# Turning q and k with DMA transposes instead of TensorE, in a sparse-attention and GEGLU kernel

## The chip, the cores and the metric

The kernel runs on one core of one Trainium2 chip. The metric is device time in microseconds (us). Each kernel was executed several times and the median is given. Ratios are the mean time of one kernel's fast runs over that of the other's fast runs of the same rounds, so they are not quite the ratio of the quoted medians. Traces come from one profiled execution; it can lie 1% away from the median. The engines are PE (TensorE), DVE (VectorE), ACT (ScalarE), POOL (GpSimd) and SP (SyncE, which issues DMAs here).

## The reference, cut to what matters

```python
B, H, S, D = 4, 8, 768, 64                  # batch, heads, tokens, head size
k_sum = k.reshape(B, H, 24, 32, D).max(axis=3)      # block keys
v_sum = v.reshape(B, H, 24, 32, D).mean(axis=3)     # block values
scores = concat([masked(q @ k.T, |i-j| < 16), q @ k_sum.T + log(32)]) # scaled by 1/8
x = softmax(scores) @ concat([v, v_sum])            # then (B*S, 512)
ffn = (gelu(x @ w_gate) * (x @ w_val)) @ w_out      # 512 -> 1536 -> 512
out = x + sigmoid(x @ w_res) * ffn
```

## The kernel before

The work is cut into eight units, two halves of 384 tokens per batch. A unit is first twelve gate/value steps (`fo_step`), then the output matmuls, between which the attention of the next unit is done. Attention needs q and k with the head size on the partitions, so they have to be turned. The turning of the next batch is spread over the twelve steps of the current batch's second half.

```python
def load_qk(src, b, parts, name):      # 96 partitions, rows of 8 tokens x 64: 2 KB runs
    t = qk.tile([PP, H, PJ, D], BF16, tag=name, name=name)
    ...
    nc.gpsimd.dma_start(out=t[...], in_=src[b, ...].rearrange("h (p j) d -> p h (j d)", j=PJ))

def turn_pair(src, hp, pool, tag):     # 16 small PE transposes into one PSUM tile
    tp = pool.tile([128, PJ, PP], BF16, tag=tag, name="tp")
    for j in range(PJ):
        for hh in range(2):
            nc.tensor.transpose(tp[hh*64:hh*64+64, j, :], src[:, 2*hp+hh, j, :], ident[0:PP, 0:PP])
    return tp

def k_step(b, hp, pool, tag):
    tp = turn_pair(k_sb[b], hp, pool, tag)
    nc.scalar.copy(kw[:, 1:NT-1, 0:BAND]..., src)           # ACT: ten windows of 96 keys
    nc.vector.tensor_copy(kw[:, 0, ...], ...)               # DVE: the two edge windows
    nc.vector.tensor_copy(kw[:, NT-1, ...], ...)
    nc.vector.tensor_reduce(out=ks..., in_=kw..., op=ALU.max)   # block keys
    nc.vector.tensor_copy(kw[:, :, BAND:BAND+NB], ks...)

def q_step(b, hp, pool, tag):
    tp = turn_pair(q_sb[b], hp, pool, tag)
    nc.scalar.copy(qT[b % 2][hp]..., tp...)

def vsum_grp(b, pool, tag):            # block means of v: 12 matmuls, then 4 small transfers
    ...
    nc.vector.tensor_copy(vpart[:], vs[:])
    for g in range(4):
        nc.sync.dma_start(out=vsum[b % 2][96+6*g:102+6*g, :], in_=vpart[32*g:32*g+6, :])

for u in range(NU):
    b, half = u // 2, u % 2
    nb = b + 1
    if half == 0 and nb < B:
        k_sb[nb] = load_qk(k, nb, 1, "k_sb")
        q_sb[nb] = load_qk(q, nb, 1, "q_sb")
        v_loads(nb)                    # 12 transfers, rows of 64 elements
    for fo in range(FO):
        fo_step(st, gvT, fo)
        if half == 1 and nb < B:
            if fo == 1:   vsum_grp(nb, ps_t, "t"); vsum_bc(...)   # POOL copies
            elif fo < 6:  k_step(nb, fo - 2, ps_t, "t")           # cut
            elif fo < 10: q_step(nb, fo - 6, ps_t, "t")           # cut
    # ... output matmuls of unit u, attention of unit u+1
```

The pool `ps_t` has one buffer, and `fo_step` takes its two PSUM tiles from a pool of four.

The softmax here doesn't subtract the row's maximum and nothing guards it: scores larger than these inputs give would overflow.

## Time and profile before

The time is 314.01 us (median of 4 runs, 311.92 to 315.53). From the page, the span, the busy times, and the chain that ended last:

```profile
span 309.7 us, 6206 instructions
PE 273.7 (88%) x2584; PEld 148.7 (48%) x2584; DVE 171.5 (55%) x379; ACT 136.0 (44%) x200; POOL 81.4 (26%) x104
PE 66%; DMA 16%; POOL 7%; DVE 5%; issue 4%; ACT 1%; POOLq 0%; DVEq 0%
```

The average of 88% hides two kinds of stage. The next view is the table of stretches: from and to, length, busy us of each engine with its instruction count, the granted PE clock, a DMA share and GB/s. The stretches are the twelve gate steps of the units 1, 2, 3 and 5; the odd units are second halves.

```profile
69.70:99.90 30.20, 25.05 (x240) 12.86 (x237) 17.14 (x32) 12.48 (x21) 13.15 (x14) 0.89 1.01 100
113.70:129.70 16.00, 16.00 (x103) 9.38 (x102) 7.92 (x15) 5.98 (x13) 0.00 (x0) 1.00 0.06 24
143.50:167.40 23.90, 21.59 (x239) 11.93 (x236) 16.38 (x32) 12.38 (x21) 12.36 (x12) 1.00 0.43 76
...
211.00:235.10 24.10, 21.62 (x241) 11.96 (x240) 16.45 (x32) 12.41 (x21) 5.58 (x3) 1.00 0.05 16
```

A second half takes 24 us where a first half takes 16. The 8 us between them are the turns, the block sums, and about 2.3 us in which PE waits for the one turning buffer. The timeline of PE shows that wait: start, length, what, and in brackets the idle time before it and what ended it.

```profile
158.64 0.53 PE L171 MATMUL tp<-ident,q_sb 96*64 96x96 bf16 x16 [1.74 <-DVE kW_3_91 L184]
```

Before the two DVE copies that free the buffer, DVE copies the block keys of the pair before:

```profile
155.93 1.91 DVE L191 COPY kW_2_90<-ks 128x288 bf16<-128x288 bf16 x1
```

The same copy took 0.23 us for the first pair. The long one lies within the three block-sum copies of POOL (152.17 to 157.75 us).

The first change of batch takes 30.2 us, 6 us longer, since PE also waits 2.7 us for v there, and its clock is 0.89 in the mean. It comes while the weights and the loads of batch 1 still keep the DMA engines full, as the chain shows (start, length, what):

```profile
48.35 17.26 DMA q_sb<-in_q_dram
67.49 8.22 DMA vext_105<-in_v_dram
75.75 1.23 PE vs L209 x8
```

### The profile page before, as it was taken

What the parts mean: (1) busy time and instruction counts of PE and PEld (TensorE: products, weight loads), DVE (VectorE), ACT (ScalarE), POOL (GpSimd) and SP (SyncE); (2) the same over time, 40 slices, a digit from 0 to 9 for tenths busy, and PEclk for the clock granted to TensorE, in tenths of its full rate; (3) what the DMA queues carried; (4) which work ended last, traced back from release to release, by engine and by line L of the source; (5) the groups of instructions that cost most, each with busy time, mean ns of one, the idle gap of its engine ahead of it and who ended that gap; (6) DMA issues with size and microseconds to landing.
All of it is one profiled execution on the core that took longest, in us unless ns stands there. A gap on an engine that the chain in (4) does not pass through costs nothing.

```text
span 309.7 us, 6206 instructions
## 1 busy us (share of the span) xinstructions
PE 273.7 (88%) x2584; PEld 148.7 (48%) x2584; DVE 171.5 (55%) x379; ACT 136.0 (44%) x200; POOL 81.4 (26%) x104
## 2 busy tenths in 40 slices
PE   1555599996979999999979999999979999999993
PEld 0521355452445455554545556555445556455641
DVE  3540764383593574367773674377863764475423
ACT  2640223641456543544547443562646623643310
POOL 8628777241393400000392400000610000000000
PEclk9975789998799999999999999999999999999998
DMA  6994999999049950001049960011000110011001
GB/s 104 163 86 51 176 196 207 207 153 149 3 67 183 101 75 35 2 34 70 5 65 178 103 111 1 2 37 68 5 0 2 36 68 2 1 65 39 2 34 68
DMA packets 54987, 22.88 MB, mean 74 GB/s; under 512 B 37480, under 2 KB 51888, under 8 KB 54960
## 3 DMA queue, kind: packets, MB, share of 16 engines
q0 software_dynamic: 51360, 16.13, 78.1%
q1 hardware_dynamic: 3600, 6.37, 6.3%
q8 instruction: 20, 0.33, 0.5%
q14 instruction: 7, 0.06, 0.1%
HBM read 32.24 MB, written 6.29 MB: 124 GB/s over the span
## 4 chain that ended last, share of the span: by engine, by line
PE 66%; DMA 16%; POOL 7%; DVE 5%; issue 4%; ACT 1%; POOLq 0%; DVEq 0%
PE f L297 18%; PE g L273 16%; PE vv L277 15%; PE r L287 6%; DMA q_sb<-in_q_dram 6%; DMA vext_104<-in_v_dram 5%; DMA w_val<-in_moe_w_val_dram 3%; PE tp L171 3%; DMA vext_105<-in_v_dram 3%; PE ao L249 2%; DVE ks L187 2%; PE s L231 2%; PE xp L260 2%; DVE gvT L281 2%; PE vs L209 1%
## 5 line engine op out<-in xcount | busy, mean ns | idle before, releaser
L281 DVE TENSOR_TENSOR gvT<-ge,vv 128x384 bf16<-128x384 f32 x96 | 52.8, 550 | 60.4 <-PE vv L277 60.3
L280 ACT ACTIVATE ge<-g 128x384 f32<-128x384 f32 x96 | 47.3, 493 | 81.1 <-PE g L273 43.9
L273 PE MATMUL g<-xT,w_gate 128*128 128x384 bf16 x384 | 81.7, 332 | 0.0
L277 PE MATMUL vv<-xT,w_val 128*128 128x384 bf16 x384 | 79.1, 329 | 0.0
L297 PE MATMUL f<-w_out,gvT 128*128 128x512 bf16 x288 | 68.4, 379 | 0.0
L277 PEld LDWEIGHTS <-w_val 128*128 128x128 bf16 x384 | 38.0, 99 | 26.5 <-issue 2.7
L235 ACT ACTIVATE P<-s,bias_t 128x768 bf16<-128x768 f32 x32 | 28.9, 904 | 45.4 <-PE s L231 45.3
L273 PEld LDWEIGHTS <-w_gate 128*128 128x128 bf16 x384 | 35.5, 99 | 25.4 <-issue 4.4
L297 PEld LDWEIGHTS <-gvT 128*128 128x128 bf16 x288 | 27.3, 98 | 31.0
L238 DVE TENSOR_TENSOR P<-P,maskt 128x768 bf16<-128x768 bf16 x32 | 17.8, 556 | 20.4 <-ACT P L235 20.4
L221 POOL COPY vext_105<-vsum_107 32x2048 bf16<-32x2048 bf16 x6 | 11.2, 1897 | 56.2 <-DMA vsum_107<-vpart 56.2
L287 PE MATMUL r<-w_res,xT 128*128 128x512 bf16 x96 | 24.8, 380 | 0.0
L96 POOL DMA_DIRECT2D vext_105<-in_v_dram x24 | 18.2, 764 | 19.6 <-DMA q_sb<-in_q_dram 7.7
L221 POOL COPY vext_104<-vsum_106 32x2048 bf16<-32x2048 bf16 (+1 forms) x4 | 8.3, 2110 | 47.5 <-DMA vsum_106<-vpart 47.4
L96 POOL DMA_DIRECT2D vext_104<-in_v_dram x24 | 18.3, 767 | 9.1 <-PE vv L277 3.5
L302 DVE SCALAR_TENSOR_TENSOR th<-th,f 128x512 f32<-128x512 f32 x24 | 16.3, 680 | 7.0 <-PE f L297 7.0
L171 PE MATMUL tp<-ident,k_sb 96*64 96x96 bf16 x256 | 9.9, 229 | 9.9 <-DMA k_sb<-in_k_dram 6.4
L255 DVE TENSOR_TENSOR xn<-ao,rz 128x384 bf16<-128x384 f32 x32 | 17.8, 558 | 1.1
L290 ACT ACTIVATE th<-r 128x512 f32<-128x512 f32 x24 | 14.3, 596 | 8.8 <-PE r L287 8.3
L304 DVE SCALAR_TENSOR_TENSOR o<-th,xn 128x512 f32<-128x512 f32 x24 | 16.6, 692 | 0.8
L249 PEld LDWEIGHTS <-P 128*64 128x64 bf16 x384 | 9.1, 114 | 14.8 <-DVE P L238 5.9
L171 PE MATMUL tp<-ident,q_sb 96*64 96x96 bf16 x256 | 9.4, 222 | 6.6 <-DMA q_sb<-in_q_dram 3.0
(150 smaller groups left out, 221.6 us busy)
## 6 DMA issues: line engine op xcount, KB each, us to landing
out_dram<-o SPq DMA_DIRECT2D x24, 256.0 KB
k_sb<-in_k_dram POOLq DMA_DIRECT2D x3, 768.0 KB, 8.0
q_sb<-in_q_dram POOLq DMA_DIRECT2D x3, 768.0 KB, 12.0
vext_104<-in_v_dram POOLq DMA_DIRECT2D x20, 96.0 KB, 8.6
vext_105<-in_v_dram POOLq DMA_DIRECT2D x20, 96.0 KB, 11.8
w_gate<-in_moe_w_gate_dram POOLq DMA_DIRECT2D x6, 256.0 KB, 8.3
w_val<-in_moe_w_val_dram POOLq DMA_DIRECT2D x6, 256.0 KB, 8.9
w_out<-in_moe_w_out_dram POOLq DMA_DIRECT2D x3, 512.0 KB, 14.0
```

The costliest lines, as they stand in the source:

```text
L96: nc.gpsimd.dma_start(out=vext[b % 2][r0:r1, t, :, 0:D], in_=src)
L171: nc.tensor.transpose(tp[hh * 64:hh * 64 + 64, j, :], src[:, 2 * hp + hh, j, :], ident[0:PP, 0:PP])
L221: eng.tensor_copy(vext[b % 2][96:128, lo:hi, :, 0:D], src)
L235: nc.scalar.activation(P.rearrange("p a t q -> p a (t q)"), s[:, :, 0:TU], AF.Exp, scale=scale, bias=bias_t[:])
L238: nc.vector.tensor_mul(Pf, Pf, maskt.unsqueeze(1).to_broadcast([128, 2 * HT, QT]))
L255: nc.vector.tensor_mul(xn, ao[:, :, :, 0:D], rz.to_broadcast([128, NSUB, 2, D]))
L273: nc.tensor.matmul(g[:, 0:TU], w_gate[:, ko, fs], st["xT"][:, ko, :], start=(ko == 0), stop=(ko == KO - 1))
L277: nc.tensor.matmul(vv[:, 0:TU], w_val[:, ko, fs], st["xT"][:, ko, :], start=(ko == 0), stop=(ko == KO - 1))
L280: nc.scalar.activation(ge[:], g[:, 0:TU], AF.Gelu)
L281: nc.vector.tensor_mul(gvT[:, fo, :], ge[:], vv[:, 0:TU])
L287: nc.tensor.matmul(r[:], st["xT"][:, ko, ss], w_res[:, ko, :], start=(ko == 0), stop=(ko == KO - 1))
L297: nc.tensor.matmul(st["f"][:], gvT[:, fo, ss], w_out[:, fo, :], start=(fo == 0), stop=(fo == FO - 1))
```

## The change

The intent is to take the turning of batches 1 to 3 off PE, ACT and DVE. k and q are loaded in token order (rows of 64 elements), and 18 DMA transposes per batch, issued from SP, write them turned into their places. As SP is then busy, the four block-sum transfers move from SP to ACT. The pool `qk` goes from two buffers to one, so the next batch's loads have to wait for these transposes. Batch 0 is left as it was.

```diff
+    def load_nat(b):
+        kn = qk.tile([BAND, NT, H, D], BF16, tag="k_nat", name="k_nat")
+        nc.gpsimd.memset(kn[0:32, 0], 0.0)
+        nc.gpsimd.memset(kn[64:96, NT - 1], 0.0)
+        for t in range(NT):
+            ...
+            nc.gpsimd.dma_start(out=kn[r0:r0 + hi - lo, t], in_=k[b, :, lo:hi, :].rearrange("h p d -> p h d"))
+        qn = qk.tile([128, S // 128, H, D], BF16, tag="q_nat", name="q_nat")
+        for c in range(S // 128):
+            nc.gpsimd.dma_start(out=qn[:, c], in_=q[b, :, c * 128:(c + 1) * 128, :].rearrange("h p d -> p h d"))
+
+    def turn_k(b, lo, hi):                      # turn_q: the same, 6 pieces of 128 x 512
+        for t in range(lo, hi):
+            nc.sync.dma_start_transpose(out=kW_all[b % 2][:, :, t, 0:BAND],
+                                        in_=k_nat[b][:, t].rearrange("p h d -> p (h d)"))
...
             for g in range(4):
-                nc.sync.dma_start(out=vsum[b % 2][96 + 6 * g:102 + 6 * g, :],
+                nc.scalar.dma_start(out=vsum[b % 2][96 + 6 * g:102 + 6 * g, :],
...
-                k_sb[nb] = load_qk(k, nb, 1, "k_sb")
-                q_sb[nb] = load_qk(q, nb, 1, "q_sb")
+                load_nat(nb)
                 v_loads(nb)
...
                 if half == 1 and nb < B:
-                    if fo == 1:
+                    if fo == 0:
+                        turn_k(nb, 0, NT)
+                        turn_q(nb, 0, S // 128)
+                    elif fo == 2:
                         vsum_grp(nb, ps_t, "t")
...
-                    elif 2 <= fo < 2 + NP:
-                        k_step(nb, fo - 2, ps_t, "t")
-                    elif 2 + NP <= fo < 2 + 2 * NP:
-                        q_step(nb, fo - 2 - NP, ps_t, "t")
+                    elif 6 <= fo < 6 + NP:
+                        k_blocks(nb, fo - 6)    # the DVE reduction and copy of k_step
```

More of the change, by code (lines that the diff above doesn't have):

```diff
@@ L51 @@
     wpool = ctx.enter_context(tc.tile_pool(name="wpool", bufs=1))
-    qk = ctx.enter_context(tc.tile_pool(name="qk", bufs=2))
+    qk = ctx.enter_context(tc.tile_pool(name="qk", bufs=1))
     work = ctx.enter_context(tc.tile_pool(name="work", bufs=3))
@@ L66 @@
     warm = const.tile([128, 512], BF16, name="warm")
-    kW = [[const.tile([128, NT, 128], BF16, name=f"kW{i}_{p}") for p in range(NP)] for i in range(2)]
-    qT = [[const.tile([128, S], BF16, name=f"qT{i}_{p}") for p in range(NP)] for i in range(2)]
+    kW_all = [const.tile([128, NP, NT, 128], BF16, name=f"kW{i}") for i in range(2)]
+    qT_all = [const.tile([128, NP, S], BF16, name=f"qT{i}") for i in range(2)]
+    kW = [[kW_all[i][:, p] for p in range(NP)] for i in range(2)]
+    qT = [[qT_all[i][:, p] for p in range(NP)] for i in range(2)]
     vext = [const.tile([128, NT, H, D + 1], BF16, name=f"vext{i}") for i in range(2)]
@@ L96, in v_loads, with turn_q @@
             nc.gpsimd.dma_start(out=vext[b % 2][r0:r1, t, :, 0:D], in_=src)
-    k_sb, q_sb = {}, {}
+    k_sb, q_sb, k_nat, q_nat = {}, {}, {}, {}
+    def load_nat(b):
[3 more added lines that the diff above has]
+        for t in range(NT):
+            lo, hi = max(0, t * QT - WIN), min(S, t * QT + QT + WIN)
+            r0 = lo - (t * QT - WIN)
+            nc.gpsimd.dma_start(out=kn[r0:r0 + hi - lo, t], in_=k[b, :, lo:hi, :].rearrange("h p d -> p h d"))
+        qn = qk.tile([128, S // 128, H, D], BF16, tag="q_nat", name="q_nat")
+        for c in range(S // 128):
+            nc.gpsimd.dma_start(out=qn[:, c], in_=q[b, :, c * 128:(c + 1) * 128, :].rearrange("h p d -> p h d"))
+        k_nat[b], q_nat[b] = kn, qn
+    def turn_k(b, lo, hi):
+        for t in range(lo, hi):
+            nc.sync.dma_start_transpose(out=kW_all[b % 2][:, :, t, 0:BAND],
+                                        in_=k_nat[b][:, t].rearrange("p h d -> p (h d)"))
+    def turn_q(b, lo, hi):
+        for c in range(lo, hi):
+            nc.sync.dma_start_transpose(out=qT_all[b % 2][:, :, c * 128:(c + 1) * 128],
+                                        in_=q_nat[b][:, c].rearrange("p h d -> p (h d)"))
     with tc.manual_schedule():
@@ L173, in turn_pair, with k_blocks @@
             return tp
+        def k_blocks(b, hp):
+            kw = kW[b % 2][hp]
+            ks = work.tile([128, NB], BF16, tag="ks", name="ks")
+            nc.vector.tensor_reduce(
+                out=ks.rearrange("d (t n) -> d t n", n=2),
+                in_=kw[:, :, WIN:WIN + QT].rearrange("d t (n w) -> d t n w", w=BLK),
+                axis=mybir.AxisListType.X, op=ALU.max)
+            nc.vector.tensor_copy(kw[:, :, BAND:BAND + NB], ks.unsqueeze(1).to_broadcast([128, NT, NB]))
         def k_step(b, hp, pool, tag):
@@ L185, in k_step @@
                                   tp[:, :, PP - 10:PP].rearrange("d j p -> d p j"))
-            ks = work.tile([128, NB], BF16, tag="ks", name="ks")
-            nc.vector.tensor_reduce(
-                out=ks.rearrange("d (t n) -> d t n", n=2),
-                in_=kw[:, :, WIN:WIN + QT].rearrange("d t (n w) -> d t n w", w=BLK),
-                axis=mybir.AxisListType.X, op=ALU.max)
-            nc.vector.tensor_copy(kw[:, :, BAND:BAND + NB], ks.unsqueeze(1).to_broadcast([128, NT, NB]))
+            k_blocks(b, hp)
         def q_step(b, hp, pool, tag):
```

## The prediction

> **What bounds the kernel now.** The page has PE busy 88% of a 309.7 us span. By the table of stretches, the twelve gate/value steps of a second half-batch (where the next batch's q and k are turned) take 24.1 us (143.7 to 167.8) and 24.3 us (211.2 to 235.4); those of a first half take 16.1 us. The 8 us between are 128 PE turns (0.47 us per 16), twelve sum matmuls (0.77 us), and 2.3 us of PE idle, because the one turning buffer waits for the ACT copy (0.96 us) and two DVE copies. The first change of batch (77.6 to 100.3) takes 22.7 us after a 2.7 us wait for v. The chain of waits shows 48 to 76 us bound by DMA: k, q, then v landing at 75.7 us.
>
> **Removed.** Per batch all turns, four 0.96 us and four 0.80 us ACT copies, eight DVE copies of 0.23 us. Best case for batches 2 and 3: 24.2 down to 17 us, 7.2 us each.
>
> **Added: loads.** k in token order has v's shape (64-element rows), q 6144 such rows. v's 12 transfers took about 10.1 us at a full queue (65.6 to 75.7), k and q 3.8 and 4.2 us. Estimate by rows: k 10.1, q 6.8, so 9 us more DMA per batch. Batches 2 and 3 hide it (loads start some 40 us early). Batch 1 does not: v lands near 84.7 us, later still if transposes hold up the engines, and PE waits at the sum matmuls. Against that stand the turns saved there. Net for batch 1: +4 us (0 to +8).
>
> **Added: transposes.** 18 in a row on SP, startable 1.8 us into the second half (after the previous unit's last store). The Trainium skill, "VectorE: DVE Perf Modes", section "The three transpose paths", gives 1309 ns for a 128x128 bf16 DMA transpose, 390 ns on TensorE; a q transfer here is four such blocks. This trace has no DMA transpose; the vsum transfers took 0.66 us of SP each. I assume about 1.1 us per k transfer, pipelined (0.4 to 2.2 possible).
>
> **The trap.** The four vsum transfers move to ACT, behind the third Gelu. By the instruction order transfers share eight completion semaphores, so ACT's fourth vsum transfer waits for the tenth k transpose (batch 1: the first q transpose). ACT is in order: later Gelus stop, and PE stops two steps later, with four PSUM buffers full. With T us per k transpose and 1.5 us to land, PE stalls about 10T-2.3 us, so a batch saves 9.5-10T (at most 7.2): a loss of 1.5 us at T=1.1. The DVE reduction at step 6 needs all k transposes, but later than that.
>
> **Sum.** 314.4+4+2x1.5 = 321 us; T may be smaller, so I put 319. Range 303 to 342. Chances: faster by over 2% 0.20, within 2% 0.36, slower by over 2% 0.44.
>
> **What would show each step.** Right: PE turns only before 16 us; batch 1's v landing at 83 to 92 us with a PE wait of 8 to 18 us at the sum matmuls; in later second halves ACT idle at the vsum transfers until a DMA into kW lands, a PE gap of several us after step 4, then no gaps; the reduction hardly waiting. Wrong: second halves of 17 us (T under 0.3), or of over 30 us ended by kW or qT transfers (T over 2).
>
> **What would make it wrong.** T above all: factor 10 per batch. Then whether transposes hold up ordinary loads, how far POOL's waits (memset of the natural k tile until its transposes end) delay the next loads, and PE's clock after a long stall.

## The result, and the profile after

The changed kernel takes 329.27 us (median of 4 runs, 327.14 to 331.19): 1.0489 times the kernel before, 95% interval 1.04 to 1.0578. Its results are correct. From the page:

```profile
span 329.5 us, 5548 instructions
PE 266.4 (81%) x2177; PEld 144.0 (44%) x2200; DVE 160.0 (49%) x355; ACT 116.0 (35%) x176; POOL 122.3 (37%) x158
PE 62%; DMA 20%; POOL 6%; SPq 4%; issue 2%; DVE 2%; ACTq 1%; ACT 1%; POOLq 0%; DVEq 0%
```

Every compute engine that was meant to be relieved is relieved: PE by 7 us, DVE by 11.5, ACT by 20. The time still grew, and the chain has a new part, "SPq", which is SP issuing transfers. The table of stretches, for the same gate steps:

```profile
71.90:105.70 33.80, 21.01 (x115) 10.35 (x113) 12.05 (x22) 5.85 (x13) 13.79 (x16) 0.80 1.40 109
119.50:135.50 16.00, 16.00 (x103) 9.38 (x101) 7.92 (x15) 5.96 (x13) 8.02 (x11) 1.00 2.91 126
149.30:179.60 30.30, 19.86 (x114) 10.47 (x113) 12.27 (x24) 5.85 (x13) 11.40 (x12) 0.77 0.56 89
...
223.20:254.70 31.50, 19.71 (x112) 10.25 (x111) 12.21 (x24) 5.83 (x13) 5.57 (x3) 0.78 0.37 74
```

The first halves did not change. The three changes of batch grew by 3.6, 6.4 and 7.4 us, where the best case for batches 2 and 3 had been 7 us less each. Their sum, 17.4 us, is most of the 19.8 us between the two traces; 2.2 us more had arisen by the start of unit 1 (71.9 against 69.7 us), a spread that other traces show too (69.7 to 71.9).

What happens in batch 2's change stands in the timeline of SP, ACT and PE, and in the chain behind it. SP first:

```profile
151.86 16.05 SPq L117 DMA_TRANSPOSE kW_88<-k_nat  x12
168.05 8.31 SPq L122 DMA_TRANSPOSE qT_90<-q_nat  x6
```

The 18 transposes keep SP busy for 24.5 us, longer than the twelve steps they were meant to hide under. ACT and PE meanwhile:

```profile
157.00 9.90 ACTq L244 DMA_DIRECT2D vsum_94<-vpart  x4
167.00 0.87 ACT L309 ACTIVATE ge<-g 128x384 f32<-128x384 f32 x2 [13.50 <-DMA kW_88<-k_nat]
167.54 1.44 PE L302 MATMUL g<-xT,w_gate 128*128 128x384 bf16 x4 [10.44 <-ACT ge L309]
```

ACT does no Gelu for 13.5 us, PE no matmul for 10.44 us, and what ends ACT's idleness is a transpose into kW, with which a Gelu has nothing to do. The chain says how that comes about (three of its pieces, then what follows):

```profile
162.32 1.20 SPq L117
...
163.62 2.58 DMA kW_88<-k_nat
...
166.22 0.68 ACTq L244
...
167.00 0.50 ACT ge L309
...
167.54 1.44 PE g L302 x4
168.98 1.28 PE vv L306 x4
...
172.82 0.96 PE g L302 x4
173.78 0.65 PE vv L306 x4
```

SP issues transpose after transpose, 1.30 us apart; the one issued at 163.62 lands 2.58 us later; in that moment ACT issues its fourth block-sum transfer, and only then its next Gelu. The compiled instruction order, condensed below, explains the coupling. In this program the transfers of SP and ACT share eight completion semaphores (DMAHW0 to DMAHW7), and a transfer that takes one waits for the previous user of it. For batch 2:

```
SP   ninth k transpose            waits DMAHW7, ...
SP   tenth k transpose            waits DMAHW0, ...      <- takes DMAHW0
ACT  vsum transfer 1              waits DMAHW1, DVE
ACT  vsum transfer 2              waits DMAHW3
ACT  vsum transfer 3              waits DMAHW6
ACT  vsum transfer 4              waits DMAHW0           <- the tenth k transpose
```

The semaphore records in the packed trace agree, and show that all four transfers wait for transposes: they are issued at 157.00, 159.69, 163.37 and 166.22 us, and the transposes that they wait for land at 156.70, 159.45, 163.20 and 166.04.

The last four lines of the chain show a second cost. After the gap, four matmuls take 1.28 us where they take 0.65 us otherwise, for about 5 us. The Trainium skill, "TensorE: Matmul & The Clock Gate", section "Part 1: The HAM clock gate", says that an idle array falls back to half its clock and gets the full one again after about 3.4 us of work; this trace agrees on the half, and the slow stretch was 5.2 us here (167.54 to about 172.8). The 14 groups from 167.54 to 179.63 us would have taken 9.1 us at 0.65 us each and took 12.1, so the stall costs 3.0 us more than its own length.

For batch 1 the timeline of PE shows the sum matmuls waiting for v:

```profile
78.59 0.38 PE L238 MATMUL vs<-vext_93,bgrp 96*32 96x512 bf16 x1 [2.03 <-DMA vext_93<-in_v_dram]
84.64 0.59 PE L238 MATMUL vs<-vext_93,bgrp 96*32 96x512 bf16 x1 [5.68 <-DMA vext_93<-in_v_dram]
88.68 0.62 PE L238 MATMUL vs<-vext_93,bgrp 96*32 96x512 bf16 x4 [3.45 <-DMA vext_93<-in_v_dram]
90.30 1.31 PE L238 MATMUL vs<-vext_93,bgrp 96*32 96x512 bf16 x5 [1.01 <-DMA vext_93<-in_v_dram]
```

The waits add up to 12.2 us; before there was one of 2.7 us.

### The profile page after: what moved, and what is told of

Same layout as the page of the kernel before. It is cut to its first block, busy times and chain, and to the rows that moved or that the text cites. A ratio compares the mean times of both kernels' runs of the same rounds, so it can differ in the third digit from the quotient of the medians.

```text
span 329.5 us, 5548 instructions
## 1 busy us (share of the span) xinstructions
PE 266.4 (81%) x2177; PEld 144.0 (44%) x2200; DVE 160.0 (49%) x355; ACT 116.0 (35%) x176; POOL 122.3 (37%) x158
## 4 chain that ended last, share of the span: by engine, by line
PE 62%; DMA 20%; POOL 6%; SPq 4%; issue 2%; DVE 2%; ACTq 1%; ACT 1%; POOLq 0%; DVEq 0%
PE g L302 17%; PE vv L306 16%; PE f L326 16%; PE r L316 6%; DMA w_out<-in_moe_w_out_dram 5%; SPq L117 4%; DMA vext_93<-in_v_dram 4%; DMA w_gate<-in_moe_w_gate_dram 3%; DMA q_nat<-in_q_dram 2%; DMA vext_92<-in_v_dram 2%; PE ao L278 2%; DMA q_sb<-in_q_dram 2%; PE s L260 2%; PE xp L289 2%; ACTq L244 1%
## 5 line engine op out<-in xcount | busy, mean ns | idle before, releaser
L302 PE MATMUL g<-xT,w_gate 128*128 128x384 bf16 x384 | 84.7, 342 | 22.7 <-ACT ge L309 22.7
L306 PE MATMUL vv<-xT,w_val 128*128 128x384 bf16 x384 | 82.1, 338 | 0.0
L326 PE MATMUL f<-w_out,gvT 128*128 128x512 bf16 x274 | 65.3, 379 | 1.5 <-issue 1.1
L302 PEld LDWEIGHTS <-w_gate 128*128 128x128 bf16 x384 | 38.6, 102 | 52.7 <-issue 32.0
L306 PEld LDWEIGHTS <-w_val 128*128 128x128 bf16 x384 | 38.8, 101 | 28.2 <-issue 5.3
L109 POOL DMA_DIRECT2D k_nat<-in_k_dram x36 | 27.2, 762 | 4.4 <-DMA w_out<-in_moe_w_out_dram 4.0
L267 DVE TENSOR_TENSOR P<-P,maskt 128x768 bf16<-128x768 bf16 x32 | 17.7, 555 | 19.7 <-ACT P L264 19.7
L112 POOL DMA_DIRECT2D q_nat<-in_q_dram x18 | 15.8, 909 | 0.2 <-issue 0.2
```

The source lines that it names most:

```text
L109: nc.gpsimd.dma_start(out=kn[r0:r0 + hi - lo, t], in_=k[b, :, lo:hi, :].rearrange("h p d -> p h d"))
L267: nc.vector.tensor_mul(Pf, Pf, maskt.unsqueeze(1).to_broadcast([128, 2 * HT, QT]))
L302: nc.tensor.matmul(g[:, 0:TU], w_gate[:, ko, fs], st["xT"][:, ko, :], start=(ko == 0), stop=(ko == KO - 1))
L306: nc.tensor.matmul(vv[:, 0:TU], w_val[:, ko, fs], st["xT"][:, ko, :], start=(ko == 0), stop=(ko == KO - 1))
L326: nc.tensor.matmul(st["f"][:], gvT[:, fo, ss], w_out[:, fo, :], start=(fo == 0), stop=(fo == FO - 1))
```

## The experiments

The theory: in batches 2 and 3 ACT stands still behind block-sum transfers that wait for transposes, transposes cost SP a fixed time per transfer, and in batch 1 v comes too late. The rivals: the transposes disturb other work wherever they run; or the whole loss is one of these parts. Eleven kernels were run, all with correct results, in four groups; each group was timed beside the kernel before on the same chip (medians 313.81, 312.33, 312.34 and 312.13 us).

| run | edit | median us | ratio to before | gate steps of units 1, 3, 5, us |
|---|---|---|---|---|
| changed kernel | | 329.27 | 1.0489 | 33.8, 30.3, 31.5 |
| e1_vsum_pool | block sums from POOL | 323.71 | 1.0303 | 33.4, 27.9, 28.2 |
| e2_turn_early | batches 2, 3 turned in the first half | 308.75 | 0.9829 | 34.2, 20.0, 18.9 |
| e3_batch1_old | batch 1 as before | 324.64 | 1.0327 | 28.6, 30.0, 30.8 |
| e4_coarse | 3 k transposes, not 12 | 311.0 | 0.9875 | 34.5, 21.7, 22.9 |
| e5_early_pool | e1 and e2 | 300.9 | 0.9599 | 32.0, 17.6, 17.7 |
| e6_hybrid | e1, e2 and e3 | 298.62 | 0.9545 | 29.7, 17.6, 17.7 |
| e7_v_first | e5, merged k, batch 1's v first | 298.06 | 0.9522 | 29.2, 16.8, 16.8 |
| e8_late_turn | batch 1's transposes after v | 335.76 | one look | 42.5, 29.0, 30.5 |
| e9_hybrid_v | e6, batch 1's v first | 295.18 | 0.9458 | 24.6, 17.6, 17.7 |
| e10_hybrid_v8 | e9, merged k, reductions later | 292.51 | 0.9395 | 22.5, 16.8, 16.8 |
| e11_before_v | kernel before, batch 1's v first | 308.79 | 0.9891 | 24.9, 25.5, 24.1 |

The profiled execution of e4_coarse counts as slow (over 1.5% above its fastest run); its stretches are read for their structure only. One of the four runs of e10 is slow too (295.12 us). At the 2% mark the changed kernel, e1 and e3 are slower than the kernel before, e4 and e11 the same, e2 unclear (interval 0.9768 to 0.9891), and e5, e6, e7, e9 and e10 faster.

### e1_vsum_pool: the wait taken off ACT

```diff
-                nc.scalar.dma_start(out=vsum[b % 2][96 + 6 * g:102 + 6 * g, :],
+                nc.gpsimd.dma_start(out=vsum[b % 2][96 + 6 * g:102 + 6 * g, :],
```

> Only edit: the four vsum transfers are issued from POOL, whose queue has its own completion semaphores, in place of ACT. My theory (ACT's wait first, the DVE reduction behind it): the 10 to 11 us ACT and PE gap after step 4 goes, but the transposes still end some 18 us into the second half, so the DVE reduction behind step 6 now waits for the twelfth k transpose, PE stops about step 9, and the second halves fall only from 30 to 31 us to 25 to 28 us; total 320 to 325. Rival (the semaphore wait on ACT is the whole loss): second halves of 17 to 18 us and a total near 303.

Measured: 323.71 us, and the second halves 27.9 and 28.2 us, as the theory said. ACT's gap is gone, and the next wait in line has taken over. DVE and then PE in the timeline of batch 2:

```profile
168.41 0.95 DVE L203 TENSOR_REDUCE ks<-kW 128x24 bf16<-128x768 bf16 x1 [8.87 <-DMA kW<-k_nat]
170.15 1.44 PE L306 MATMUL vv<-xT,w_val 128*128 128x384 bf16 x4 [8.02 <-DVE gvT L310]
```

The reduction behind step 6 needs all twelve k transposes, and SP issues the last of these some 18 us into the second half. Removing a wait was worth only the distance to the next one: about 3 us of a gap of 10 to 12.

### e2_turn_early: the transposes moved, ACT left alone

```diff
+                if half == 0 and 2 <= nb < B and fo == 6:
+                    turn_k(nb, 0, NT)
+                    turn_q(nb, 0, S // 128)
                 if half == 1 and nb < B:
-                    if fo == 0:
+                    if fo == 0 and nb < 2:
```

> Only edit: for batches 2 and 3 the 18 transposes are issued at step 6 of the first half, when their data has landed, in place of step 0 of the second half; vsum transfers stay on ACT with the same semaphores; batch 1 as it was. My theory (transposes cost nothing by themselves, only what waits for them): second halves of batches 2 and 3 fall to 17 to 18.5 us, first halves stay at 16 us, total 302 to 306. Rival (transposes disturb the engines or the ordinary transfers wherever they run): the first halves grow by several us, and the total stays above 312.

Measured: 308.75 us. The rival falls: the 18 transposes were issued from 122.2 to 148.5 us, through the rest of the first half, and it did not grow. Its gate steps took 15.9 us (first line), and from its start to that of the second half it took 29.8 us, as in the kernel before (113.7 to 143.5). The total is 3 us above my range, because the second halves kept up to 2 us that I had not counted:

```profile
119.70:135.60 15.90, 15.90 (x100) 9.28 (x96) 7.92 (x15) 5.89 (x13) 6.29 (x9) 1.00 2.33 140
149.50:169.50 20.00, 17.24 (x112) 9.41 (x108) 13.30 (x22) 5.77 (x13) 9.78 (x10) 1.00 0.23 49
```

```profile
155.46 2.87 ACTq L244 DMA_DIRECT2D vsum<-vpart  x4
158.43 0.87 ACT L309 ACTIVATE ge<-g 128x384 f32<-128x384 f32 x2 [4.76 <-DMA vsum<-vpart]
158.97 0.81 PE L302 MATMUL g<-xT,w_gate 128*128 128x384 bf16 x4 [1.70 <-ACT ge L309]
```

With no transpose left to wait for, four issues in a row still hold ACT for 2.87 us, more than the lead that four PSUM buffers give PE.

### e3_batch1_old: batch 1 alone restored

```diff
-                load_nat(nb)
+                if nb == 1:
+                    k_sb[nb] = load_qk(k, nb, 1, "k_sb")
+                    q_sb[nb] = load_qk(q, nb, 1, "q_sb")
+                else:
+                    load_nat(nb)
                 v_loads(nb)
...              # and k_step, q_step, vsum_grp of the kernel before where nb == 1
```

> Batch 1 loaded and turned as in the kernel before (2 KB rows, PE turns), batches 2 and 3 as changed. My theory (batch 1 costs 4 to 6 us net through the late v): total 3 to 6 us under the changed kernel, 323 to 326, batch 1's gate stretch back from 33.7 to about 30 us and v landing near 76 us. Rival (the whole loss sits in batches 2 and 3): total within 1.5 us of the changed kernel.

Measured: 324.64 us, 1.0327 of before against the changed kernel's 1.0489. That is 1.6% or 5 us, though from another group of runs. Batch 1's stretch fell to 28.6 us and the last wait for v ended at 77.2 us. So between a fifth (3.6 of the 17.4 us by which the stretches grew) and a third (5 of 15 us) of the loss sits in batch 1, the rest in batches 2 and 3.

### e4_coarse: fewer and larger transposes

```diff
-    kW_all = [const.tile([128, NP, NT, 128], BF16, name=f"kW{i}") for i in range(2)]
+    kW_all = [const.tile([128, NT, NP, 128], BF16, name=f"kW{i}") for i in range(2)]
...
-        for t in range(lo, hi):
-            nc.sync.dma_start_transpose(out=kW_all[b % 2][:, :, t, 0:BAND],
-                                        in_=k_nat[b][:, t].rearrange("p h d -> p (h d)"))
+        for t in range(lo, hi, 4):
+            nc.sync.dma_start_transpose(
+                out=kW_all[b % 2][:, t:t + 4, :, 0:BAND].rearrange("x t p r -> x (t p) r"),
+                in_=k_nat[b][:, t:t + 4].rearrange("p t h d -> p (t h d)"))
```

> The 12 k transposes per batch are merged into 3 of 96 rows by 2048 columns (k tiles of a window kept side by side, same bytes); q stays at 6. Fixed cost per transfer (24 and 32 blocks of 16 by 128 both took about 1.2 us of SP): k takes about 4 us of SP instead of 16, the ACT gap falls under 2 us, second halves 17 to 20 us, total 303 to 310. Cost per block: each of the three takes about 5 us, k as a whole still about 16 us, ACT's gap shrinks to some 2 to 5 us since fewer transfers share its semaphores, but the DVE reduction waits, second halves 24 to 30 us, total 318 to 329.

Measured: 311.0 us (fast runs 309.57 to 311.52). The same bytes of k now hold SP for 5.75 us instead of 16.05:

```profile
152.60 5.75 SPq L117 DMA_TRANSPOSE kW<-k_nat  x3
158.46 8.63 SPq L123 DMA_TRANSPOSE qT<-q_nat  x6
```

For comparison, the single transposes of the changed kernel, as the view of their source lines gives them (shortest, median and longest duration in ns):

```profile
L117 SPq DMA_TRANSPOSE kW_88<-k_nat x12: 1180/1197/1446, 151.9 to 166.5; - x12
L122 SPq DMA_TRANSPOSE qT_90<-q_nat x6: 1188/1216/1391, 168.1 to 175.1; - x6
```

A k transfer has 24 blocks of 16 by 128 elements, a q transfer 32, and both take 1.2 us. So, with few loads running, the cost is nearly all per transfer: from 1.34 us (16.05 / 12) for 24 blocks to 1.92 us (5.75 / 3) for 96, a block adds about 8 ns. Among loads it is another matter. In batch 1 of this run the three merged transposes held SP for 15.05 us (the twelve single ones of the changed kernel 17.07 us), and in e10, where they are issued in the first half, for 13.35 us (against 17.39 us for the twelve single ones in e2). The second halves (21.7 and 22.9 us) and the total are a little above what I expected for this theory, since PE still waits 2.4 and 3.1 us for ACT, and its matmuls take twice their time for some 3 to 5 us after each wait. In batch 2 ACT issued its block-sum transfers between 155.9 and 159.5 us, while the second and third k transposes and the first q transpose were being issued. So ACT can issue beside transposes in flight; what stopped it in the changed kernel was the semaphore that it had to wait for.

### e5_early_pool: both remedies

The edits of e1 and e2 together.

> Both edits together: transposes of batches 2 and 3 at step 6 of the first half, and vsum transfers from POOL. Theory: what was left of the wait in the early-turn run (second halves of 20.0 and 18.9 us) was ACT busy issuing four vsum transfers of 0.68 us each; without them second halves of 17 to 18 us, total 303 to 306. Rival (the rest is the DVE reductions crowding the Gelu products, not ACT): second halves stay at 19 to 20 us, total 307 to 309.

Measured: 300.9 us, faster than expected, and the second halves at 17.6 and 17.7 us with PE at full clock:

```profile
146.30:163.90 17.60, 17.10 (x112) 9.45 (x109) 12.84 (x22) 5.88 (x12) 10.07 (x11) 1.00 0.17 55
```

The rest in e2 was ACT, not DVE. The changed kernel, with its transposes issued earlier and four small transfers on another queue, is 4% faster than the kernel before.

### e6_hybrid: batch 1 restored too

The edits of e1, e2 and e3 together.

> As the run before, and batch 1 loaded and turned as in the kernel before. If the costs add: batch 1 gives back the 5 us that it gave in the run with batch 1 alone restored (its gate stretch 28.6 against 33.7 us), so 298 to 301, faster than the kernel before by 4 to 5%.

Measured: 298.62 us, inside the range. Batch 1's stretch is 29.7 against 32.0 us in e5, so in this combination it gives back 2.3 us, less than the 5 us of e3.

### e7_v_first: the first need loaded first

```diff
+                if nb == 1:
+                    v_loads(nb)
+                    load_nat(nb)
+                else:
+                    load_nat(nb)
+                    v_loads(nb)
...              # with the edits of e1, e2, e4, and the reductions at steps 8 to 11
```

> Early turns, vsum from POOL, k transposes merged to 3, the reductions from step 8, and in batch 1 v is loaded ahead of k and q, which stay in token order and are turned by DMA. Theory (batch 1's cost is only that v, needed first, lands last): v lands by 70 to 76 us, no or a short wait at the sum matmuls, k lands about 78 us and its three transposes end by 84 to 88 us; batch 1's gate stretch 20 to 25 us in place of 33.7, total 290 to 298. Rival (the DMA engines are the limit there and some operand is always late): stretch of 28 us or more, total 300 or above.

Measured: 298.06 us, just above my range, and batch 1's stretch of 29.2 us is far from the 20 to 25 that I had expected. There the rival was right about the stretch (28 us or more), though not about the total (300 or above). v's wait vanished, and the wait moved to k:

```profile
73.26 12.70 SPq L117 DMA_TRANSPOSE kW<-k_nat  x3
95.69 0.95 DVE L204 TENSOR_REDUCE ks<-kW 128x24 bf16<-128x768 bf16 x1 [11.57 <-DMA kW<-k_nat]
```

The third merged transpose was issued at 83.74 us, when its loads had landed, and took 11.83 us to land (both from the chain). The view of the source line of the merged transposes ends with their time from issue to landing (shortest, median and longest, in us). For e4 and then for e7 it is:

```profile
DMA to landing us min/median/max: 5.0/5.0/13.2
```

```profile
DMA to landing us min/median/max: 10.2/11.8/14.9
```

In e4 only batch 1's transposes ran in a stretch full of loads, and the median is 5.0 us. In e7 those of batches 2 and 3 were also issued while the loads of q or v were running, and all took 10 us and more. The changed kernel shows the same within one row of transposes: by its semaphore records the first seven k transposes of batch 1 landed after 8.2 to 9.9 us, and the q transposes, issued once v had landed, after 2.5 to 3.2 us. Transposes are slow beside ordinary loads here.

### e8_late_turn: what makes v late

```diff
-                nc.scalar.dma_start(out=vsum[b % 2][96 + 6 * g:102 + 6 * g, :],
+                (nc.sync if b == 1 else nc.scalar).dma_start(out=vsum[b % 2][96 + 6 * g:102 + 6 * g, :],
...
-                    if fo == 0:
+                    if fo == (3 if nb == 1 else 0):
                         turn_k(nb, 0, NT)
```

> The changed kernel, but in batch 1 the vsum transfers go back to SP ahead of the transposes, so no transpose runs before v has landed. Not meant to be fast (the reductions of batch 1 then wait for late transposes, total 335 to 345). It tells what makes v late: if the extra rows of k and q alone, v's last window still lands at 88 to 91 us; if transposes in flight hold up the ordinary loads, it lands at 79 to 84 us.

Measured: one look, so a run of unknown state, 335.76 us, as slow as expected. SP issued no transpose before 89.2 us, and the last wait for v ended earlier:

```profile
83.91 1.44 PE L238 MATMUL vs<-vext,bgrp 96*32 96x512 bf16 x9 [2.45 <-DMA vext<-in_v_dram]
```

Counted from the start of the stretch, to take out the spread of the starts, v was complete after 6.1 us before (75.75 - 69.7), after 14.0 us here (83.91 - 69.9), and after 18.4 us in the changed kernel (90.30 - 71.9). Token order thus delays v by about 8 us (from this one run). Against the changed kernel the transposes in flight would add about 4, but e1, e2, e4 and e5, which also have them in flight there, give 18.1, 15.2, 19.2 and 16.7 us (from the start of the stretch to the end of PE's last wait for v). So they add 1 to 5 us, against a single run; that the hold-up goes both ways is likely, and not shown beyond this spread.

### e9_hybrid_v and e10_hybrid_v8: versions that beat both

e9 is e6 with batch 1's v loaded ahead of its k and q (which have 2 KB runs and PE turns again). e10 adds the merged k transposes of e4, and the reductions at steps 8 to 11 in place of 6 to 9.

```diff
                 if nb == 1:
+                    v_loads(nb)
                     k_sb[nb] = load_qk(k, nb, 1, "k_sb")
                     q_sb[nb] = load_qk(q, nb, 1, "q_sb")
                 else:
                     load_nat(nb)
-                v_loads(nb)
+                    v_loads(nb)
```

> The hybrid (batch 1 loaded and turned as in the kernel before, batches 2 and 3 by early DMA transposes, vsum from POOL), with batch 1's v loaded ahead of its k and q. If v's 3 us wait at the sum matmuls goes without a new wait for k: batch 1's gate stretch 26 to 28 us in place of 29.7, total 295 to 297. If k and q then arrive late for the turns (they land some 10 us later), the stretch stays at 29 us or grows, total 298 or above.

> The same, with the k transposes of batches 2 and 3 merged to 3 and the reductions from step 8 in place of 6. In the v-first run these gave second halves of 16.8 us in place of 17.6, so 1.6 us under the run before in this call: 293.5 to 296. If the reductions' place does not matter, the two runs are equal.

Measured: 295.18 us, inside the range with a shorter stretch than expected, and 292.51 us, 1 us below the range, with ratios of 0.9458 (0.9389 to 0.9527) and 0.9395 (0.9306 to 0.9483). e10's page and table of stretches:

```profile
PE 84%; DVE 5%; DMA 5%; issue 1%; POOL 1%; ACT 1%; POOLq 0%; DVEq 0%
```

```profile
69.90:92.30 22.40, 21.74 (x239) 11.92 (x236) 15.96 (x32) 12.37 (x21) 13.85 (x16) 1.00 0.68 99
135.90:152.70 16.80, 16.80 (x113) 9.45 (x110) 10.61 (x20) 5.93 (x13) 9.32 (x11) 1.00 0.06 22
```

A second half now takes the 16 us of a first half and the 0.8 us of the sum matmuls, and nothing else; the chain is 84% PE. e10 also lies 2 us lower in batch 1 (22.5 against 24.6), in a stretch that neither of its two edits is aimed at. The traces show where: in e9 two block-key copies of DVE took 1.20 and 1.91 us beside POOL's block-sum copies, and PE then waited 1.04 and 1.83 us for the turning buffer; in e10 POOL's copies came 1.2 us later in the stretch, and PE had no such wait. No run tells whether the edits caused that, and the two ratios' intervals overlap.

### e11_before_v: a control without DMA transposes

The kernel before, with `v_loads(1)` ahead of the two `load_qk` calls of batch 1.

> Control without any DMA transpose: the kernel before, with batch 1's v loaded ahead of its k and q and nothing else changed. If the order of batch 1's loads is worth what the last call suggests (gate stretch 24.6 in place of 29.7 us), the total is 306 to 310, and the rest of the gain of the best version, some 14 to 16 us, is due to the DMA transposes of batches 2 and 3 and their placement. If it comes near 298, most of that gain was never due to the transposes.

Measured: 308.79 us, 0.9891 of before, with batch 1's stretch at 24.9 us. So 3 us of e10's gain have nothing to do with transposes, and some 16 us (308.79 - 292.51, from two groups of runs) separate the two kernels. About 2.4 of these lie in batch 1 (24.9 against 22.5), which both turn on PE; the rest comes from the DMA transposes of batches 2 and 3 and where they stand.

## Why the prediction was right, point by point

- **Total and direction.** 319 us with a range of 303 to 342 was predicted, and slower as the likeliest class; 329.27 us was measured, slower by 4.9%. Right, with a centre 10 us too low. The range is 39 us wide, so that the time fell into it says little: the kernel lost 15 us where the sum had 7, and the chance given to slower was 0.44.
- **The trap.** Right in every part that the trace can show: ACT idle at the block-sum transfers until a transfer into kW lands, PE stopped two steps later, no gaps after it. e5 removes it, and the second halves fall to 17.6 us.
- **T, the time per k transpose.** 1.1 us was assumed, 1.30 us was measured. With it the stated formula, 10T - 2.3, gives a stall of 10.7 us; 10.44 and 11.79 us were measured. The landing, assumed at 1.5 us, is near it only if counted from the end of the issue: the tenth transpose of batch 2 held SP for 1.45 us (the longest in the view of L117) and landed 1.1 us after that, 2.58 us after its start.
- **The mis-sized terms.** The loss per batch was put at 1.5 us; 6.4 and 7.4 us were measured. The stall is 1.7 to 3.1 us longer than at T = 1.1 (8.7 us), and PE's half clock after it costs 3.0 us (worked out for batch 2). The clock was named as a risk and not put into the sum. Moving the centre from 321 to 319 was in the wrong direction. The second halves of 30.3 and 31.5 us, ended by a kW transfer, even met what the prediction had named as a sign against it (over 30 us, T over 2), although T was only 1.30. The prediction's own terms at that T give 24.2 + 3.5 = 27.7 us, and the half clock's 3.0 us make it 30.7.
- **The page's 1309 ns.** Read as a time per 128 by 128 block, it would have given an estimate of over 5 us per q transfer (4 x 1.309). The transfers overlap: each cost SP 1.2 us, with 24 or with 32 blocks, and a q transfer landed after 2.5 us (median in e4).
- **Batch 1.** +4 us was predicted; its stretch grew by 3.6, and restoring batch 1 gave about 5 us back in e3 and 2.3 in e6. v was to land near 84.7 us, later if transposes held up the engines: 83.9 without transposes in flight (e8, one run) and 90.3 with them.
- **"The DVE reduction at step 6 needs all k transposes, but later than that."** Right, and e1 shows it: with ACT's wait away, it is the next one, at 8 to 9 us.

## What to carry to other kernels

A DMA transpose takes work off PE, but 18 of them hold the issuing engine for about 24 us, and that has to end before its first reader; issue them as soon as their data has landed. Merging small ones took k's part from 16 to 6 us where few loads ran, and only from 17 to 13 us among loads. Before moving a small transfer to an engine that computes, look at what its completion semaphore waits for: an in-order engine passes a wait on to everything behind it. When a wait is found, find the next one as well, since removing the first (e1) gave 6 us of 329, moving the transposes (e2) about 20, and both (e5) some 28.

## What the Trainium skill lacked or had wrong

- "VectorE: DVE Perf Modes", section "The three transpose paths", gives one duration, 1309 ns for 128 by 128. That section lacks the split: with few other transfers running, SP was held 1.20 us by a transfer of 96 by 512, 1.22 us by 128 by 512, and 1.92 us by 96 by 2048, and a transfer landed 2.6 us (96 by 512) or 5.0 us (96 by 2048) after its issue. Among loads, one of 96 by 2048 held SP for up to 5.3 us (e10).
- "Advanced Engine Details and Errata", section "X-Bar Transpose (TRN2)", says that transpose DMAs are as fast as regular ones and expects 350 to 400 GB/s. In pieces of 96 by 512, k's 1.18 MB (12 x 96 x 512 x 2 bytes) took 16.05 us of SP, which is 73 GB/s; in pieces of 96 by 2048 (e4) they took 5.75 us, which is 205 GB/s. Both are the rates at which SP issued, not what the DMA engines could move.
- "DMA: Bandwidth & Descriptors", section "Rules for kernel authors", says that a transpose next to ordinary DMAs needs nothing. For the results that is so (all runs were correct). In time the transposes were held up: those of 96 by 2048 landed after 5.0 us with few loads beside them and after 10.2 to 14.9 us among loads. That the loads are held up too is only likely: v came 1 to 5 us later in the runs with transposes in flight than in the one without (e8).
- No page read tells why the k windows landed 4.0 us after issue (median) and the v windows, with the same source shape, after 8.1 to 8.8. The destinations differ (v's rows lie 65 elements apart), and v's loads are issued last, behind those of k and q; no run tested either.
